# Experts of a routed MLP in steps of 256 tokens, layer 1 with the weights held still, instead of blocks of 128 tokens

## The chip, the cores and the metric

One core of one Trainium2 chip runs the whole program. The metric is the device time of one execution in microseconds (us); the time of a kernel is the median of several runs. Beside it one execution is profiled: its trace gives each instruction's engine, start and length. The engines are PE (TensorE; PEld is its loading of weights), DVE (VectorE), ACT (ScalarE), POOL (GpSimd) and SP, which only issues transfers.

## The reference

Three parts follow each other: attention, a plain MLP, and an MLP of eight experts, of which each token uses one. The change is in the last and at its seam to the second.

```python
def _moe_ref(x, w_in, w_out):                       # 2304 x 512, hidden 2048
    r = np.maximum(x @ w_in, 0.0)
    return (r * r) @ w_out

def _moe2_ref(x, expert_emb, tau, w1, w2):          # 8 experts, 512 -> 1024 -> 512
    xn, en = x / norm(x), expert_emb / norm(expert_emb)
    logits = xn @ en.T / tau
    expert_idx = np.argmax(logits, axis=1)
    gate_w = softmax(logits)[arange(N), expert_idx]
    for e in range(E):
        mask = expert_idx == e
        h = np.maximum(x[mask] @ w1[e], 0.0)
        out[mask] = gate_w[mask, None] * (h @ w2[e])
```

The inputs are drawn with a fixed seed. Worked out with the reference, the tokens per expert are 676 (expert 4), 436 (5), 449 (7), 466 (0), 171 (1) and 106 (2); experts 3 and 6 get none. The kernel visits them in that order.

## The kernel before

**Numbers.** Every float32 product is made of three single-pass products of rounded halves: a tensor is split into a high part (`hh`, `xTh`, `Wh`), a rounded copy made by ACT, and a low part (`hl`, `xTl`, `Wl`), the difference made by DVE. "hi times hi, hi times lo, lo times hi" is why matmuls come in threes.

**The plain MLP, second half of its hidden layer.** Chunks `cc` of 256 tokens; the last chunk comes first, then 0 to 7. `layer1` (L680) holds a 128x128 piece of the weights still and streams 256 tokens through it, 12 matmuls a step; `layer2` (L714 to L716) holds the hidden values and streams 512 columns of weights, 6 matmuls a step. Each finished chunk is routed while the next one is computed (`route`): DVE works out the expert of each token, its place among that expert's tokens (`lj`), and POOL makes a one-hot table `L` of the places (L860). After four routed chunks `first_block` picks the expert with the most tokens so far as the first one, loads its weights, and collects the first 128 of its tokens into `xg[0]` with an indirect transfer (L922). PE transposes them five steps later (L927).

**Tables.** After the last chunk `tables` turns counts and places into lists of token numbers: DVE builds `Bk` and `rg`, PE multiplies them with `L` (L1047), and `T.idxg` tells the indirect transfers which rows to collect. A later part (L1107 to L1123, run at `next(gates)`, then L1127 on PE) makes the gate weight of each token the same way.

**Experts.** A block (`body`) is 128 tokens of one expert. With `xT` (the transposed tokens) held still, layer 1 streams `w1` in 24 matmuls of 512 columns (L1240) into two banks; ACT takes the ReLU into `h` (L1259, L1265); PE transposes `h` in two lots of four (L1229); ACT and DVE split it; layer 2 holds the transposed `h` and streams `w2` in 24 matmuls of 512 columns (L1250 to L1252). In between, four transposes of the next block's tokens (L1183). Each of the 21 blocks is stored with a DVE multiply by the gate (L1307) and an indirect transfer to the output (L1308). When the expert changes, 16 half pieces of weights are split by ACT and DVE (`own`, `ahead`), under conditions that each engine evaluates for itself. Two copies of the body stand in the program, one for each of two weight slots; PE, ACT and DVE run in the order of the code.

**Order of blocks 0 to 2.** Block 0 stands before the tables in PE's order only in part: the last chunk's routing and the tables lie among its matmuls. `next(gates)` is called after block 1.

Of the kernel before, what the change touches and what calls it, by code (L numbers as in the profile page):

```python
# [9 lines left out]
F32 = DT.float32  # L10
F32R = DT.float32r
BF16 = DT.bfloat16
I32 = DT.int32
# [17 lines left out]
NBLK = 25  # L31
NSURE = 18
# [26 lines left out]
TURN0 = 5  # L59
# [554 lines left out]
class Mlp:  # L614
# [158 lines left out]
    def routing(self, c, late, emb, tau):  # L773
# [8 lines left out]
        self.sq = c.tile([128, DM], BF16, name="sq")  # L782
# [18 lines left out]
    def route(self, cc, x2):  # L801
# [51 lines left out]
        V.tensor_reduce(rk, t16, AX.X, ALU.add)  # L853
        ri = c.tile([128, 2, 2], I32, name="ri", tag="ri")
# [17 lines left out]
    def first_block(self):  # L872
# [36 lines left out]
        for sl in spans:  # L909
            V.scalar_tensor_tensor(b0[:, sl], R.lj[:, 1, sl], 0.0, R.O[:, sl, 0], ALU.is_equal, ALU.mult)  # L910
            V.tensor_scalar_mul(rhs[:, sl, 0], b0[:, sl], R.iotap)
            V.tensor_tensor(rhs[:, sl, 1], b0[:, sl], R.iotat[:, sl, 0], ALU.mult)
        tab = R.ps.tile([128, 512], F32, name="tab0", tag="r")
        tiles = [t for sl in spans for t in range(sl.start, sl.stop)]
        for t in tiles:
            nc.tensor.matmul(tab[:, :2], R.L[:, t], rhs[:, t], start=t == tiles[0], stop=t == tiles[-1])
        p1 = c.tile([128, 1], F32, name="p1")
        V.tensor_scalar(p1, tab[:, 0:1], -1.0, None, ALU.add)
        idx = c.tile([128, 1], I32, name="idx0")
        V.scalar_tensor_tensor(idx, tab[:, 1:2], 128.0, p1, ALU.mult, ALU.add)  # L920
        m = len(tiles) * 128
        nc.gpsimd.indirect_dma_start(sh.xg[0], None, sh.x2d[:m], IO(ap=idx, axis=0), bounds_check=m - 1, oob_is_err=False)  # L922
        for _ in range(TURN0):
            yield
        pt = self.psr.tile([128, 512], F32, name="xt", tag="xt", bufs=2)
        for kc in range(4):
            nc.tensor.transpose(pt[:, kc * 128:kc * 128 + 128], sh.xg[0][:, kc * 128:kc * 128 + 128], sh.ident)  # L927
        sh.xT0 = [c.tile([128, DM], F32R, name=n) for n in ("xT0h", "xT0l")]
        split(nc, pt, *sh.xT0, nc.scalar, nc.vector)
        yield  # L930

# [30 lines left out]
def routing_setup(tc, sh, c):  # L962
# [20 lines left out]
    R.iotat = c.tile([128, NTT, NBLK], BF16, name="iotat")  # L983
    for a, n, base in ((0, NTT - 2, 2), (NTT - 2, 2, 0)):
        nc.gpsimd.iota(R.iotat[:, a:a + n], [[1, n], [0, NBLK]], base=base, channel_multiplier=0,
                       allow_small_or_imprecise_dtypes=True)

    R.two = c.tile([128, NBLK], I32, name="two")
    nc.gpsimd.iota(R.two, [[1, NBLK]], base=126, channel_multiplier=0)
# [8 lines left out]
def tables(ctx, tc, sh):  # L998
# [5 lines left out]
    T.idxg = c.tile([128, NBLK], I32, name="idxg")  # L1004
    T.idxs = c.tile([128, NBLK], I32, name="idxs")
    T.gate = c.tile([128, NBLK], F32, name="gate")
    T.meta = c.tile([128, NBLK + 4], I32, name="meta")
# [7 lines left out]
    V.tensor_scalar(ci, cnt[:, :E], 127.0, None, ALU.add)  # L1015
    V.tensor_scalar(ci, ci, 7, None, ALU.arith_shift_right)
# [4 lines left out]
    for t in cum:  # L1021
# [15 lines left out]
    V.tensor_tensor(sb, sb, R.lj[:, 1], ALU.add)  # L1037
    Bk = st.tile([128, NTT, NBLK], BF16, name="Bk")
    V.tensor_tensor(Bk, R.iota128[:, :NBLK].unsqueeze(1).to_broadcast([128, NTT, NBLK]),
                    sb.unsqueeze(2).to_broadcast([128, NTT, NBLK]), ALU.is_equal)  # L1040
    rg = st.tile([128, NTT, 3, NBLK], BF16, name="rg")
    rhs = rg[:, :, :2]
    V.tensor_scalar_mul(rhs[:, :, 0], Bk, R.iotap)
    V.tensor_tensor(rhs[:, :, 1], Bk, R.iotat, ALU.mult)
    tab = pst.tile([128, 512], F32, name="tab", tag="r")
    for i in range(NTT):
        nc.tensor.matmul(tab[:, :2 * NBLK], R.L[:, i], rhs[:, i].rearrange("p a b -> p (a b)"),  # L1047
                         start=i == 0, stop=i == NTT - 1)
    P1 = st.tile([128, NBLK], F32, name="P1")
    V.tensor_copy(P1, tab[:, :NBLK])  # L1050
    idx = st.tile([128, NBLK], F32, name="idx")
    V.scalar_tensor_tensor(idx, tab[:, NBLK:2 * NBLK], 128.0, P1, ALU.mult, ALU.add)
    first = V.tensor_scalar(T.idxg, idx, -1.0, 0.0, ALU.add, ALU.max)
    for s in range(1, 2):
        nc.gpsimd.indirect_dma_start(sh.xg[s], None, sh.x2d, IO(ap=T.idxg[:, s:s + 1], axis=0),
                                     bounds_check=NT - 1, oob_is_err=False)
    with tc.issue_after(first.ins):
        ge = st.tile([128, NBLK, E], F32, name="ge")
        V.tensor_tensor(ge, R.iota128[:, :NBLK].unsqueeze(2).to_broadcast([128, NBLK, E]),
                        cend.unsqueeze(1).to_broadcast([128, NBLK, E]), ALU.is_ge)  # L1060
        ex = st.tile([128, NBLK], F32, name="ex")
# [5 lines left out]
        V.tensor_tensor(ge, ge, used.unsqueeze(1).to_broadcast([128, NBLK, E]), ALU.mult)  # L1067
        at = st.tile([128, NBLK], F32, name="at")
# [3 lines left out]
        V.tensor_tensor(ge, at.unsqueeze(2).to_broadcast([128, NBLK, E]), rank.unsqueeze(1).to_broadcast([128, NBLK, E]),  # L1072
                        ALU.is_equal)
        flags = st.tile([128, 3, NBLK], F32, name="flags")
        V.memset(flags[:, :, 0], 0.0)
        more = st.tile([128, NBLK], F32, name="more")
        V.tensor_reduce(more, ge, AX.X, ALU.add)
        V.tensor_tensor(ge, ge, R.iota128[:, :E].unsqueeze(1).to_broadcast([128, NBLK, E]), ALU.mult)
        nx = st.tile([128, NBLK], F32, name="nx")
        V.tensor_reduce(nx, ge, AX.X, ALU.add)  # L1080
        e8 = st.tile([128, NBLK], I32, name="e8")
        V.tensor_scalar(e8, nx, R.e0, None, ALU.add)
        V.tensor_scalar(T.meta[:, :NBLK], e8, E - 1, None, ALU.bitwise_and)
# [8 lines left out]
        V.tensor_tensor(flags, flags, R.two.bitcast(F32).unsqueeze(1).to_broadcast([128, 3, NBLK]), ALU.mult)  # L1092
# [11 lines left out]
    with tc.issue_after(last.ins):  # L1104
# [29 lines left out]
def experts(tc, sh, gates, w1, w2, out):
    nc = tc.nc
    T = sh.T
    with ExitStack() as ctx:
        st = ctx.enter_context(tc.tile_pool(name="est", bufs=1, reuse_waits="tile"))
        psh = [sh.psm.tile([128, 512], F32, name=f"psh{j}", tag="y", bufs=2) for j in range(2)]
        pst = [sh.psm.tile([128, 512], F32, name="pst0", tag="L1", bufs=1)]  # L1140
        pst += [sh.psr.tile([128, 512], F32, name=f"pst{j}", tag="xt", bufs=2) for j in range(1, 3)]
        psy = [sh.psr.tile([128, 512], F32, name=f"psy{j}", tag="y", bufs=2) for j in range(2)]
        ident = sh.ident
# [3 lines left out]
        def ring(n, name, shape, dtype, tiles=(), used=0):  # L1147
            tiles = [*tiles] + [st.tile(shape, dtype, name=f"{name}{j}") for j in range(len(tiles), n)]
            turns = [used]
            rings.append(turns)  # L1150

            def take():
                turns[0] += 1
                return tiles[(turns[0] - 1) % n]
            return take

        new_xh = ring(2, "xTh", [128, DM], F32R, sh.xT0[:1], 1)
        new_xl = ring(2, "xTl", [128, DM], F32R, sh.xT0[1:], 1)
        new_h = ring(1, "h", [128, F], F32)
        new_hh = ring(2, "hh", [128, 512], F32R)  # L1160
        new_hl = ring(2, "hl", [128, 512], F32R)
        spare = sh.x1[NCH - 1].rearrange("p a b -> p (a b)")
        new_psh = ring(2, "psh", None, None, psh)
        new_pst = ring(3, "pst", None, None, pst)
        new_psy = ring(2, "psy", None, None, psy)

        xg, xT, hb = {}, {}, {}

        def gather(s):
            if s >= NBLK:  # L1170
                return
            t = sh.xg[s % 2]
            nc.gpsimd.indirect_dma_start(t, None, sh.x2d, IO(ap=T.idxg[:, s:s + 1], axis=0),  # L1173
                                         bounds_check=NT - 1, oob_is_err=False)
            xg[s] = t

        def turn_x(s):
            if s >= NBLK:
                return
            t = xg.pop(s)  # L1180
            pt = new_pst()
            for kc in range(4):
                nc.tensor.transpose(pt[:, kc * 128:kc * 128 + 128], t[:, kc * 128:kc * 128 + 128], ident)  # L1183
            hi = new_xh()
            lo = new_xl()
            xT[s] = (hi, lo)
            return split(nc, pt, hi, lo, nc.scalar, nc.vector)
# [251 lines left out]
```

## Time and profile before

| | |
|---|---|
| median of 3 runs | 978.58 us (978.37 to 980.16) |
| profiled execution, its own time | 976.67 us |
| its span in the trace | 974.7 us |
| PE busy | 924.9 us, 95% of the span |
| DVE, ACT, POOL busy | 63%, 57%, 29% |
| expert part, from the first layer 1 matmul | 691.9 us to the end |
| indirect stores | 21 |

A matmul's bar in the trace is longer than the time it takes its place in the row: the next one starts before the bar has ended. The cost of a matmul is read from the distance of the starts. Times below are us from the start of the span.

### The profile page before, as it was taken

The page shows a single profiled execution, that of the slowest core. Times are in us where ns is not written, and L with a number is a line of the kernel's source. Part 1 is how long each engine was busy: PE and PEld are TensorE (multiplying, and loading weights), DVE is VectorE, ACT ScalarE, POOL GpSimd, SP SyncE. Part 2 cuts the span into 40 slices and gives each one's busy share as a digit, 9 for nine tenths or more (in the row PEclk, how much of TensorE's full clock was granted, in tenths as well). Part 3 has the DMA queues.
Part 4 walks back from the last instruction along what each step waited for, and adds up shares of the span by engine and source line. Part 5 has one row for each costly group of instructions (what it writes and reads, how often), then busy time and mean ns, then how long its engine had stood idle before and what let it go on. Part 6 is the DMA issues. An engine that isn't in the chain of part 4 may idle for free. (4 is left out here: it accounts for less than half of the span.)

```text
span 974.7 us, 19052 instructions
## 1 busy us (share of the span) xinstructions
PE 924.9 (95%) x5864; PEld 772.3 (79%) x5864; DVE 615.6 (63%) x1741; ACT 553.8 (57%) x1425; POOL 278.6 (29%) x346
## 2 busy tenths in 40 slices
PE   7887798899999999999999999999989999999996
PEld 6666675688888888898888988898777878887875
DVE  4797768656676765488517778888642444444364
ACT  4676767677676766576655555664422434444353
POOL 4364554533333443101111112441412111111121
PEclk8999989899999999999999999999999999999998
DMA  6676655454444430254311112421061342425160
GB/s 165 148 177 149 156 138 143 99 127 94 117 95 115 95 85 2 67 171 154 109 44 44 64 46 92 158 66 44 23 218 46 92 154 85 173 73 185 66 204 28
DMA packets 106779, 105.10 MB, mean 108 GB/s; under 512 B 65967, under 2 KB 76207, under 8 KB 106624
## 3 DMA queue, kind: packets, MB, share of 16 engines
q1 hardware_dynamic: 101200, 90.17, 33.2%
q0 software_dynamic: 4224, 12.89, 3.9%
q8 instruction: 58, 0.95, 0.4%
q14 instruction: 97, 0.79, 0.3%
q10 hardware_dynamic: 1200, 0.30, 0.1%
HBM read 70.01 MB, written 14.43 MB: 87 GB/s over the span
## 5 line engine op out<-in xcount | busy, mean ns | idle before, releaser
L680 PE MATMUL ps<-xh,Wh 128*128 128x256 f32 x416 | 119.7, 288 | 0.0
L392 POOL TENSOR_SCALAR A<-A,sm,g 128x512 f32<-128x512 f32 (+4 forms) x108 | 75.4, 706 | 153.3 <-DVE sm L455 60.9
L680 PE MATMUL ps<-xl,Wh 128*128 128x256 f32 x416 | 118.3, 284 | 0.9 <-DVE xl L654 0.9
L680 PE MATMUL ps<-xh,Wl 128*128 128x256 f32 x416 | 118.1, 284 | 0.0
L714 PE MATMUL y<-Wh,gh 128*128 128x512 f32 x288 | 115.3, 400 | 0.1
L716 PE MATMUL y<-Wh,gl 128*128 128x512 f32 x288 | 113.6, 394 | 0.0
L715 PE MATMUL y<-Wl,gh 128*128 128x512 f32 x288 | 113.4, 394 | 0.0
L446 ACT ACTIVATE A<-A,nm 128x256 f32<-128x256 f32 (+2 forms) x144 | 80.3, 558 | 37.8 <-DVE nm L438 36.8
L690 DVE TENSOR_TENSOR gl<-r,gh 128x256 fp32r<-128x256 f32 x144 | 69.5, 483 | 46.2 <-ACT gh L689 41.7
L684 ACT ACTIVATE r<-ps 128x256 f32<-128x256 f32 x144 | 54.8, 380 | 76.5 <-PE ps L680 73.1
L438 DVE CUSTOM_DVE_ANT_0 A<-ps,mask 64x256 f32<-64x256 f32 (+4 forms) x160 | 75.5, 473 | 33.7 <-PE ps L431 30.9
L109 DVE TENSOR_TENSOR hl<-pst,hh 128x512 fp32r<-128x512 f32 x42 | 29.0, 691 | 104.4 <-ACTq L1215 93.6
L680 PEld LDWEIGHTS ps<-xh,Wh 128*128 128x128 f32 x416 | 79.7, 192 | 4.9 <-issue 1.9
L680 PEld LDWEIGHTS ps<-xl,Wh 128*128 128x128 f32 x416 | 79.8, 192 | 3.8 <-DVE xl L654 1.1
L680 PEld LDWEIGHTS ps<-xh,Wl 128*128 128x128 f32 x416 | 79.9, 192 | 0.0
L689 ACT CAST gh<-r 128x256 fp32r<-128x256 f32 x144 | 58.4, 405 | 37.6 <-PE y L715 35.5
L1308 POOL DMA_INDIRECT out_dram<-x,idxs x21 | 21.2, 1011 | 197.1 <-DVE x L1307 149.4
L1250 PE MATMUL psy<-Wh,hh 128*128 128x512 f32 x168 | 70.2, 418 | 0.0
L1252 PE MATMUL psy<-Wh,hl 128*128 128x512 f32 x168 | 66.8, 398 | 0.4 <-DVEq L1215 0.4
L108 ACT CAST Wh<-x 128x512 fp32r<-128x512 f32 x96 | 55.0, 618 | 20.5 <-SPq L1297 7.9
L1251 PE MATMUL psy<-Wl,hh 128*128 128x512 f32 x168 | 66.4, 395 | 0.0
L716 PEld LDWEIGHTS y<-Wh,gl 128*128 128x128 f32 x288 | 54.1, 188 | 13.6 <-DVE gl L690 0.7
(333 smaller groups left out, 2426.6 us busy)
## 6 DMA issues: line engine op xcount, KB each, us to landing
x<-in_moe_w_dram SPq DMA_DIRECT2D x48, 512.0 KB, 3.8
raw<-in_moe_w_in_dram SPq DMA_DIRECT2D x16, 512.0 KB, 4.1
raw<-in_moe_w_out_dram SPq DMA_DIRECT2D x16, 512.0 KB, 4.0
ks<-hk SPq DMA_DIRECT2D x60, 128.0 KB, 2.4
x2d<-x SPq DMA_DIRECT2D x18, 256.0 KB, 2.0
kn<-in_k_dram SPq DMA_DIRECT2D x32, 128.0 KB, 2.8
vn<-in_v_dram SPq DMA_DIRECT2D x32, 128.0 KB, 2.7
x2p<-x SPq DMA_DIRECT2D x16, 256.0 KB, 2.4
```

Of the source, the lines that this page charges most:

```text
L392: nc.gpsimd.tensor_scalar(A, A, a, b, ALU.mult, ALU.mult)
L438: nc.vector.tensor_tensor_reduce(A[rows, a:n], tiles[j][rows, :w], mask[rows, end - w:end], -1.0, 3e38, ALU.add, ALU.min, nm[rows, j:j + 1])
L446: nc.scalar.activation(A[:, a:a + w], src, AF.Exp, bias=nm[:, 0:1], scale=sign, accum_out=sm[:, i:i + 1])
L680: nc.tensor.matmul(ps[:, :CH], a, b, start=n == 0, stop=n == len(ops) - 1)
L689: self.later(3, "act", lambda: nc.scalar.copy(gh, r))
L690: self.later(3, "dve", lambda: nc.vector.tensor_tensor(gl, r, gh.bitcast(F32), ALU.subtract))
L714: nc.tensor.matmul(y, gh[:, sl], wh, start=first, stop=False)
L715: nc.tensor.matmul(y, gh[:, sl], wl, start=False, stop=False)
L716: nc.tensor.matmul(y, gl[:, sl], wh, start=False, stop=last)
L1250: nc.tensor.matmul(y, hh[:, sl], a, start=n == 0 and kc == 0, stop=False)
L1251: nc.tensor.matmul(y, hh[:, sl], b, start=False, stop=False)
L1252: nc.tensor.matmul(y, hl[:, sl], a, start=False, stop=n == 1 and kc == 3)
```

## The change

A step is now 256 tokens of one expert, two halves of 128. In layer 1 the pieces of `w1` are held still and the 256 transposed tokens stream through, so that `h` arrives transposed; ACT takes the ReLU straight into the high part, DVE the low part straight from the bank, and the transposes of `h`, the tile `h` and the copies of its transposes are gone. Layer 2 is as before, for two halves, into two fixed banks `y[0]` and `y[1]`. There is one pair of `xT` tiles instead of two in turn. Tables have 34 columns (17 steps of two halves) instead of 25; with the token counts above there are 3 + 2 + 2 + 2 + 1 + 1 = 11 steps instead of 6 + 4 + 4 + 4 + 2 + 1 = 21 blocks. The first step has both halves: `first_block` collects 128 tokens after four routed chunks and 128 more after seven (`SEEN`), transposed three MLP steps later. If the first expert had under 256 tokens by then, `hole` moves its later tokens on; with the inputs above it has 486 and `hole` is 0. `next(gates)` is now called ahead of step 0, and the conditions' words are read at the end of step 0.

```diff
-NBLK = 25
-NSURE = 18
+NST = 17
+NHB = 2 * NST
+NSURE = 9
+SEEN = 7
...
+        def fetch(half):
...
+            for t in tiles:
+                nc.tensor.matmul(tab[:, :2], R.L[:, t], rhs[:, t], start=t == tiles[0], stop=t == tiles[-1])
+            p1 = c.tile([128, 1], F32, name=f"p1_{half}")
+            V.tensor_scalar(p1, tab[:, 0:1], -1.0, None, ALU.add)
...
+            nc.gpsimd.indirect_dma_start(sh.xg[half], None, sh.x2d[:m], IO(ap=idx, axis=0), bounds_check=m - 1,
+                                         oob_is_err=False)
...
+        fetch(0)
         for _ in range(TURN0):
             yield
...
+        turn(0)
+        while R.count < SEEN:
+            yield
+        cnt = R.ps.tile([128, 512], F32, name="cnt", tag="r")
+        nc.tensor.matmul(cnt[:, :E], R.ones, R.Osum[:, SEEN - 1], start=True, stop=True)
+        V.tensor_scalar(R.hole[:, 0:1], cnt[:, 0:1], -1.0, float(CH), ALU.mult, ALU.add)
+        V.tensor_scalar_max(R.hole[:, 0:1], R.hole[:, 0:1], 0.0)
+        fetch(1)
+        for _ in range(TURN1):
+            yield
+        turn(1)
         yield
+
+
+def turned(nc, sh, pt, half):
+
+    for kc in range(4):
+        nc.tensor.transpose(pt[:, kc * 128:kc * 128 + 128], sh.xg[half][:, kc * 128:kc * 128 + 128], sh.ident)
+    hi, lo = (t[:, :, half * 128:half * 128 + 128] for t in sh.xT)
+    split(nc, pt.rearrange("p (k t) -> p k t", k=4), hi, lo, nc.scalar, nc.vector)
...
+            def layer1(g):
+                ps = new_bank().rearrange("p (a b) -> p a b", a=2)
+                for a in range(2):
+                    sl = slice((2 * g + a) * 128, (2 * g + a) * 128 + 128)
+                    for kc in range(4):
+                        for j, (w, x) in enumerate(((Wh, hi), (Wh, lo), (Wl, hi))):
+                            nc.tensor.matmul(ps[:, a], w[kc][:, sl], x[:, kc], start=kc + j == 0, stop=kc + j == 5)
+                hh, hl = hT[g] = new_hh(), new_hl()
+                nc.scalar.activation(hh, ps, AF.Relu)
+                nc.vector.scalar_tensor_tensor(hl, ps, 0.0, hh.bitcast(F32), ALU.max, ALU.subtract)
+
+            def layer2(g):
+                hh, hl = hT[g]
+                for a in range(2):
+                    wh, wl = Wh[4 + g][:, a * 512:a * 512 + 512], Wl[4 + g][:, a * 512:a * 512 + 512]
+                    for h in range(2):
+                        xh, xl = hh[:, a, h * 128:h * 128 + 128], hl[:, a, h * 128:h * 128 + 128]
+                        nc.tensor.matmul(y[h], xh, wh, start=g + a == 0, stop=False)
+                        nc.tensor.matmul(y[h], xh, wl, start=False, stop=False)
+                        nc.tensor.matmul(y[h], xl, wh, start=False, stop=g + a == 4)
+
+            own(4)
+            layer1(0)
+            own(5)
+            layer1(1)
+            own(6)
+            layer2(0)
+            own(7)
+            layer2(1)
+            if s == 0:
+                words["once"] = nc.values_load(T.once[0:1], engines=[ENG.Activation, ENG.DVE], min_val=0, max_val=1)
+            ahead(0)
+            layer1(2)
+            ahead(1)
+            layer1(3)
+            ahead(2)
+            layer2(2)
+            if s + 1 < NST:
+                for h in range(2):
+                    turned(nc, sh, pst[h], h)
+            ahead(3)
+            layer2(3)
...
         load(range(8), 0)
...
+        next(gates)
+        block(0)
         with tc.manual_schedule(engines={ENG.PE, *IN_ORDER}):
...
+            for h in range(2):
+                nc.scalar.copy(room(0, h), y[h])
+            block(1)
             next(gates, None)
```

**Three places in the engines' orders.** PE in the second half of an ordinary block, before (`h` is the tile of ReLU values, `xg` the collected tokens of the next block, `hh` and `hl` the split parts):

```order
L1229 MATMUL pst_9288<-ident,h_9294 128x128 x4
L1250 MATMUL psy_9290<-Wh_5_76,hh_9295 128x512
L1251 MATMUL psy_9290<-Wl_5_84,hh_9295 128x512
L1252 MATMUL psy_9290<-Wh_5_76,hl_9297 128x512
L1250 MATMUL psy_9290<-Wh_5_76,hh_9295 128x512
L1215 UNCONDITIONAL_BRANCH
L1221 UNCONDITIONAL_BRANCH
L1251 MATMUL psy_9290<-Wl_5_84,hh_9295 128x512
L1252 MATMUL psy_9290<-Wh_5_76,hl_9297 128x512
L1183 MATMUL pst_9289<-ident,xg_6593 128x128 x4
L1250 MATMUL psy_9290<-Wh_6_77,hh_9296 128x512
L1251 MATMUL psy_9290<-Wl_6_85,hh_9296 128x512
```

PE at the same point of an ordinary step, now:

```order
L1255 MATMUL psy_9340<-Wh_6_77,hh_9342 128x512
L1256 MATMUL psy_9340<-Wl_6_85,hh_9342 128x512
L1257 MATMUL psy_9340<-Wh_6_77,hl_9344 128x512
L961 MATMUL pst_9337<-ident,xg_6592 128x128 x4
L961 MATMUL pst_9338<-ident,xg_6593 128x128 x4
L1255 MATMUL psy_9339<-Wh_7_78,hh_9343 128x512
L1256 MATMUL psy_9339<-Wl_7_86,hh_9343 128x512
L1257 MATMUL psy_9339<-Wh_7_78,hl_9345 128x512
L1255 MATMUL psy_9340<-Wh_7_78,hh_9343 128x512
```

The transposes of `h` are gone, and those of the next tokens have become two lots, one for each half.

DVE around the gate weights, before: the low part of the next block's tokens (`xT0l`), then the conditions of the weight pieces, then the gate arithmetic between blocks 1 and 2.

```order
L109 TENSOR_TENSOR xT0l<-pst_9289,xT0h 128x512
L1221 COMPARE_AND_BRANCH
L109 TENSOR_TENSOR Wl_3_82<-x_3_93,Wh_3_74 128x512
L1221 UNCONDITIONAL_BRANCH x2
L1283 UNCONDITIONAL_BRANCH
L936 TENSOR_SCALAR sq<-ss 128x18
L937 TENSOR_SCALAR sq<-sq 128x18
L939 RECIPROCAL sq<-sq 128x18
L940 SCALAR_TENSOR_TENSOR sq<-sq,ss 128x18
L941 SCALAR_TENSOR_TENSOR sq<-sq 128x18
```

DVE near the end of step 0, now: the arithmetic of the gates (`gr`, `gp`, `rg`) stands around the low parts of both halves of step 1's tokens (`xTl`).

```order
L1153 TENSOR_TENSOR gr<-gt,gp 128x18
L1158 TENSOR_TENSOR rg<-Bk,gp 128x18x34
L1154 CAST gp<-gr 128x18
L111 TENSOR_TENSOR xTl<-pst_9337,xTh 128x4x128
L1234 COMPARE_AND_BRANCH
L111 TENSOR_TENSOR Wl_3_5685<-x_3_93,Wh_3_5677 128x512 x2
L1234 UNCONDITIONAL_BRANCH x2
L1155 TENSOR_TENSOR gr<-gr,gp 128x18
L1158 TENSOR_TENSOR rg<-Bk,gp 128x18x34
L1156 CAST gp<-gr 128x18
L111 TENSOR_TENSOR xTl<-pst_9338,xTh 128x4x128
L1158 TENSOR_TENSOR rg<-Bk,gp 128x18x34
```

The gate arithmetic has moved from between blocks 1 and 2 to in among the two `xTl`, which step 1's first matmuls read.

PE in the plain MLP just after the seventh chunk is routed, before (`gh` and `gl` are hidden values of the plain MLP):

```order
L680 MATMUL ps<-xh_8736,Wl_0_5682 128x256
L714 MATMUL y<-Wh_7_5681,gh 128x512
L715 MATMUL y<-Wl_7_5689,gh 128x512
L716 MATMUL y<-Wh_7_5681,gl 128x512
L714 MATMUL y<-Wh_7_5681,gh 128x512
```

and now, with the first of 14 matmuls of the second `fetch`:

```order
L682 MATMUL ps<-xh_8739,Wl_0_5682 128x256
L716 MATMUL y<-Wh_7_5681,gh 128x512
L717 MATMUL y<-Wl_7_5689,gh 128x512
L926 LDWEIGHTS L
L926 MATMUL tab_8844<-rhs_8043,L 128x2
```

What moved in is the table of the second half: it reads `rhs` and `L`, which DVE and POOL make from the seventh chunk's places.

## Rows read from the trace of the kernel before

**Rows 1.** The page, costliest groups: line, engine, operation, count, busy, mean ns.

```profile
L680 PEld LDWEIGHTS ps<-xh,Wh 128*128 128x128 f32 x416 | 79.7, 192 | 4.9 <-issue 1.9
...
L1308 POOL DMA_INDIRECT out_dram<-x,idxs x21 | 21.2, 1011 | 197.1 <-DVE x L1307 149.4
```

**Rows 2.** Windows: stretch, length, busy and count by engine, PEclk, DMA.

```profile
790.00:890.00 100.00, 99.24 (x478) 80.62 (x477) 41.88 (x64) 41.06 (x72) 17.42 (x16) 1.00 0.36 122
```

**Rows 3.** Timeline of PE in block 4: start, length, instruction, idle before.

```profile
752.49 0.40 PE L1240 MATMUL psh<-Wh,xT0h 128*128 128x512 f32 x1
...
756.23 0.39 PE L1240 MATMUL psh<-Wl,xT0h 128*128 128x512 f32 x1
756.46 0.60 PE L1229 MATMUL pst<-ident,h 128*128 128x128 f32 x4
...
757.13 0.39 PE L1240 MATMUL psh<-Wh,xT0h 128*128 128x512 f32 x1
```

**Rows 4.** Timeline of PE: the first layer 1 matmul of blocks 7 and 14.

```profile
790.20 0.40 PE L1240 MATMUL psh<-Wh,xTh 128*128 128x512 f32 x1
...
877.48 0.39 PE L1240 MATMUL psh<-Wh,xT0h 128*128 128x512 f32 x1
```

**Rows 5.** Timeline of PE: the first and last of 12 matmuls in the plain MLP.

```profile
677.64 0.28 PE L680 MATMUL ps<-xh,Wh 128*128 128x256 f32 x1
...
678.95 0.28 PE L680 MATMUL ps<-xh,Wl 128*128 128x256 f32 x1
```

**Rows 6.** PE's waits from 692 to 967: total us, times, longest.

```profile
PE pst L1183 <- DMA xg<-x2d,idxg: 2.3, 1, 2.3
PE pst L1229 <- ACT h L1259: 2.1, 4, 0.8
PE psh L1240 <- DVE lj L858: 0.8, 1, 0.8
PE psy L1252 <- DVEq L1215: 0.4, 1, 0.4
```

**Rows 7.** Windows after the wait for the tokens of block 1.

```profile
710.20:713.60 3.40, 3.40 (x10) 2.62 (x9) 2.21 (x9) 0.43 (x1) 0.60 (x1) 0.50 0.42 106
713.60:720.00 6.40, 6.40 (x31) 5.28 (x31) 0.69 (x1) 1.90 (x4) 0.00 (x0) 1.00 0.94 337
```

**Rows 8.** Timeline of PE in the same stretch.

```profile
710.38 0.63 PE L1250 MATMUL psy<-Wh,hh 128*128 128x512 f32 x1
...
712.93 0.63 PE L1240 MATMUL psh<-Wh,xTh 128*128 128x512 f32 x1
```

**Rows 9.** Timeline when the seventh chunk is routed.

```profile
666.16 0.18 PE L845 MATMUL pr<-O,tri 128*128 128x16 bf16 x1 [1.19 <-DVE O L840]
...
667.98 0.17 DVE L858 CAST lj<-ri 128x4 f32<-128x4 int32 x1
...
668.25 1.18 POOL L860 TENSOR_SCALAR L<-iota,lj 128x128 bf16<-128x128 f32 x2 [2.26 <-DVE lj L858]
```

**Rows 10.** Timeline in block 0: the table's 18 matmuls.

```profile
703.80 0.61 PE L1047 MATMUL tab<-rg,L 128*128 128x50 bf16 x18
```

**Rows 11.** Timeline of DVE: the gate arithmetic, its first and last rows.

```profile
727.25 0.18 DVE L1107 TENSOR_SCALAR ss<-ss 128x18 f32<-128x18 f32 x1
...
730.25 1.70 DVE L1123 TENSOR_TENSOR rg<-Bk,gp 128x450 bf16<-128x450 bf16 x3
```

**Rows 12.** Waits from 730 to 975: DVE's sequencer at a condition.

```profile
DVE xTl L109 <- DVEq L1221: 0.8, 5, 0.2
```

**Rows 13.** Timeline in block 4: the next block's tokens.

```profile
761.73 0.60 PE L1183 MATMUL pst<-ident,xg 128*128 128x128 f32 x4
...
762.37 0.59 ACT L108 CAST xTh<-pst 128x512 fp32r<-128x512 f32 x1 [1.18 <-PE pst L1183]
...
762.99 0.69 DVE L109 TENSOR_TENSOR xTl<-pst,xTh 128x512 fp32r<-128x512 f32 x1 [1.07 <-ACTq L1221]
```

**Rows 14.** Timeline of the end.

```profile
966.39 0.39 PE L1252 MATMUL psy<-Wh,hl 128*128 128x512 f32 x1
...
966.82 0.75 DVE L1307 TENSOR_SCALAR x<-psy,gate 128x512 f32<-128x512 f32 x1 [1.23 <-PE psy L1252]
...
967.85 1.01 POOL L1308 DMA_INDIRECT out_dram<-x,idxs  x1 [10.16 <-DVE x L1307]
```

More of the change, by code (lines that the diff above doesn't have):

```diff
@@ L56 @@
 STRICT, BUSY = 9, {-5: 14, 0: 12, 2: 6}
-TURN0 = 5
+TURN0, TURN1 = 5, 3
 ONPE = (NCH - 2,)
@@ L923, in first_block, with turn @@
+        def turn(half):
+            pt = self.psr.tile([128, 512], F32, name="xt", tag="xt", bufs=2)
+            turned(nc, sh, pt, half)
+        fetch(0)
         for _ in range(TURN0):
             yield
[L925 to L928, printed above, removed]
@@ L1177, in turn_x @@
[L1177 to L1187, printed above, removed]
+            for n in range(2):
+                nc.gpsimd.indirect_dma_start(sh.xg[n], None, sh.x2d, IO(ap=T.idxg[:, 2 * s + n:2 * s + n + 1], axis=0),
+                                             bounds_check=NT - 1, oob_is_err=False)
@@ L1278, in block, with arms @@
+            ahead(3)
+            layer2(3)
+        def arms(s, flag, *does):
+            kept = [list(r) for r in rings]
+            with tc.If(bit(words[flag], s) < 1) as cmp, tc.manual_schedule(engines=IN_ORDER | {ENG.PE}):
+                does[0]()
+            for r, was in zip(rings, kept):
+                r[:] = was
+            with cmp.Else(), tc.manual_schedule(engines=IN_ORDER | {ENG.PE}):
+                does[1]()
         def block(s):
-            kept = [list(r) for r in rings], dict(xg), dict(xT)
@@ L1293, in block @@
-            if s + 1 < NBLK:
-                with tc.If(bit(more, s + 1) > 0):
+                body(0, 0)
+                words["odd"] = word(0, [ENG.PE, ENG.Activation, ENG.DVE])
+                words["change"] = word(1, [ENG.Activation, ENG.DVE])
+                words["more"] = word(2, [ENG.SP])
+            else:
+                arms(s, "odd", lambda: body(s, 0), lambda: body(s, 1))
+            if s + 1 < NST:
+                with tc.If(bit(words["more"], s + 1) > 0):
                     load(range(4), s + 1)
@@ L1296, in block @@
             if s:
-                with tc.If(bit(more, s) > 0):
+                with tc.If(bit(words["more"], s) > 0):
                     load(range(4, 8), s)
             gather(s + 2)
-            return y
-        def room(s):
-            return spare[:, s % 2 * DM:s % 2 * DM + DM]
-        def store(s, y):
-            ob = room(s)
-            nc.vector.tensor_scalar_mul(ob, y, T.gate[:, s:s + 1])
-            nc.gpsimd.indirect_dma_start(out, IO(ap=T.idxs[:, s:s + 1], axis=0), ob, None,
-                                         bounds_check=NT - 1, oob_is_err=False)
@@ L1311, in experts, with room, store @@
-        xT[0] = sh.xT0
-        xg[1] = sh.xg[1]
+        def room(s, h):
+            return rooms[s % 2][:, h * DM:h * DM + DM]
+        def store(s, src):
+            for h in range(2):
+                ob, c = room(s, h), 2 * s + h
+                nc.vector.tensor_scalar_mul(ob, src[h], T.gate[:, c:c + 1])
+                nc.gpsimd.indirect_dma_start(out, IO(ap=T.idxs[:, c:c + 1], axis=0), ob, None,
+                                             bounds_check=NT - 1, oob_is_err=False)
         load(range(8), 0)
-        once = nc.values_load(T.once[0:1], engines=[ENG.PE, ENG.Activation, ENG.DVE], min_val=0, max_val=1)
@@ L1315, in experts @@
-        change = word(1, [ENG.Activation, ENG.DVE])
-        more = word(2, [ENG.SP])
-        y = block(0)
+        next(gates)
+        block(0)
         with tc.manual_schedule(engines={ENG.PE, *IN_ORDER}):
-            nc.scalar.copy(room(0), y)
-            y = block(1)
-            nc.scalar.copy(room(1), y)
-            next(gates)
-            odd = word(0, [ENG.PE, ENG.Activation, ENG.DVE])
-            y = block(2)
-            next(gates, None)
-        store(0, room(0))
-        store(1, room(1))
@@ L1334, in experts @@
         with ExitStack() as ifs:
-            for s in range(NSURE, NBLK):
+            for s in range(NSURE, NST):
                 ifs.enter_context(tc.If(nbv > s))
-                store(s, block(s))
+                block(s)
+                store(s, y)
 @with_exitstack
@@ L1404, in tile_kernel @@
             pass
+        for _ in sh.R.first:
+            pass
     gates = tables(ctx, tc, sh)
```

258 lines of the change are left out of this document (96 added, 162 removed).

## The prediction

> **What bounds the kernel now.** I read the windows first. In a long stretch of blocks PE is busy 99 us of 100 at the full granted clock, the other engines less than half [rows 2]. So time there is what PE's own instructions need, plus the few waits, and the question is how many instructions of which kind a token costs. The timeline gives the price of each kind. Sixteen matmuls of 512 columns lie between 752.49 and 756.23, so one takes 0.234 us. From 756.23 to 757.13 there are two of them and four transposes; the four take 0.43 [rows 3]. A block is 48 matmuls and twelve transposes: 48 x 0.234 + 3 x 0.43 = 12.5. Seven blocks in a row took 87.28, 12.47 each [rows 4], so that sum is complete: branches between blocks cost PE nothing that can be seen.
>
> The list of PE's waits has what comes on top. In blocks 1 to 20 they are 2.1 us before the transposes of `h`, four times, and 0.4 once; in block 0 0.8 behind the last chunk's places and 2.3 behind the collected tokens of block 1 [rows 6]. A matmul's bar is 0.39 where its turn is 0.234, so each wait costs 0.16 more than is listed. After the 2.3 us the clock stood at half for one stretch [rows 7], where matmuls came 0.425 apart (six from 710.38 to 712.93, [rows 8]).
>
> **The change, part by part.**
>
> *Steps for blocks, -3.2.* Layer 1 of a step is 96 matmuls of 256 columns with weights still. The plain MLP has this form already: twelve of them lie 0.119 apart (1.31 over eleven, [rows 5]), the same 128x256 with a 128x128 load of the same type. So 96 x 0.119 = 11.43; layer 2 is 48 x 0.234 = 11.22; eight transposes 0.87: 23.52 a step. Eleven steps are 258.7; the 21 blocks of now, seen as 21 stores [rows 1], are 21 x 12.47 = 261.9. Taking out 16 of 24 transposes for 256 tokens is worth 1.7 a pair, but 0.2 goes to the narrower matmuls, and 22 halves are computed for 21 blocks, which takes back half a step.
>
> Narrow matmuls double the weight loads of layer 1. A load lasts 0.192 [rows 1], more than the 0.119 between matmuls, so it lies beside other matmuls and costs nothing. The Trainium skill says otherwise (TensorE: Matmul & The Clock Gate, Part 3, "The mechanism"): a load overlaps running matmuls only if it goes to other rows of the array, and here both use all 128. The trace does not agree: starts 0.119 apart with loads of 0.192 can't stand one behind the other. What it would cost if the rule held for the added loads is a rival below.
>
> *Waits in blocks 1 to 20, -3.3.* The 2.1 and 0.4, five times with 0.16 each. The longest ones come from ACT being late with the first ReLU, behind eight weight pieces at a change of expert. Now two pieces stand between ReLUs, and each ReLU (0.6) and low part (0.75, as the multiply in [rows 14]) has 24 matmuls, 2.86 us, to be done in. If that cover failed the 3.3 would come back. Bounds: 0 to 3.3.
>
> *Block 0's waits, -4.7.* 0.8 + 2.3 + 2 x 0.16 = 3.4, and seven matmuls at half clock, 7 x 0.19 = 1.3. They go because a full pair of tokens, 23.5 us of matmuls, now stands where 12.5 did: the table of step 1 and its two collections have ten more us. Bounds: 3.0 to 4.7.
>
> *Table of step 0, +0.6.* It lies in layer 2 of step 0 and needs three DVE operations that are now 34/25 as wide; three such took 1.70 [rows 11], so they grow by 0.6, and its 18 matmuls (0.61, [rows 10]) by at most 0.2. Part of it is covered. 0 to 1.2; I take the middle.
>
> *Start of step 1, +3.8.* This is a wait that the change makes. DVE's order puts the gate arithmetic ahead of and between the two `xTl`, where it stood behind them. From the last matmul of layer 1 in step 0: about 1.75 until the fourth `hl` is made (0.3, a ReLU 0.6, 0.75 and handovers). Then two small operations 0.42, the arithmetic from L1107 to the first `rg` 3.0 [rows 11], two `rg` of 0.57 x 34/25 = 0.77 each, three conditions of about 0.2 [rows 12], two `xTl` of 0.69 [rows 13]: 6.95, so 8.7 in all. PE has 24 matmuls of layer 2, eight transposes and one matmul of step 1 in that time, 5.62 + 0.87 + 0.12 = 6.6. It waits 2.1, and 2.5 if DVE comes half a us late from the table's arithmetic ahead of it, which I take. A wait of 2.3 was followed by half clock before, so 1.3 more. Bounds: 0 (other order of arrival, no slowdown) to 5.5 (DVE 1.5 later). The matmuls of step 1 are what stands behind it; reading the condition's word on PE falls into the same wait and is free there.
>
> *Second fetch in the plain MLP, +2.4.* After the seventh chunk's `pr` at 666.3 PE has twelve matmuls and two of layer 2 until the new table: 1.9, so it is there at 668.2. Its last one-hot `L` ends at 668.25 + 1.18 = 669.4 [rows 9], 669.7 with the two operations for `hole` ahead of `lj`. Wait 1.5. The 14 matmuls take 14/18 of 0.61, 0.5; four transposes 0.43. The other instructions queue on DVE (some ten of 0.2, one of 0.69) inside a chunk that had room. The transposes come some 6.5 us after the table (four large matmuls at 0.234 and two MLP steps of 12 x 0.119 + 6 x 0.234); until then three small operations on DVE, an issue of 1.01 on POOL [rows 14] and the landing must be done. No row prices that landing alone; I take it to fit, and the upper bound holds a miss of some 1.5. Bounds: 0.9 to 4 (the clock falls too).
>
> *End, +0.5.* The last step stores two halves: one more multiply of 0.75 and one more issue of 1.01 on POOL [rows 14], of which the first store's landing covers most, since expert 2 has 106 tokens and the second half is empty. 0 to 1.1.
>
> *At nothing.* One `xT` pair instead of two: layer 1 has read it long before it is rewritten. At a step's end the second half's cast ends 0.64 + 2 x 0.6 after the first transpose and its low part 0.75 later, 2.6, while PE has 0.87 + 2.81 + 0.12 = 3.8: 1.2 to spare; the rival below is about that. One pair of `y` banks: two multiplies of 0.75, needed 5.7 later. POOL issues the same number of halves and is busy 17 us of 100 [rows 2]. Weight transfers are as many as before and have twice the time per step.
>
> Sum: -3.2 - 3.3 - 4.7 + 0.6 + 3.8 + 2.4 + 0.5 = -3.9. The profiled execution spans 974.7 and took 976.67; it would span 970.8 and take 972.8. The median of the runs is 978.58, 1.9 above the profiled one; less 3.9 it is **974.7**.
>
> **Rivals.**
>
> *The gates don't hold step 1.* If DVE gets through faster than I add up, or the wait is short enough for the clock to stay, 3.8 goes: 970.9; with the MLP's wait gone too, 969.4. For it: the sum of small operations is long and each may overlap by 0.1. Against: two `rg` and both `xTl` alone are 2.9, in strict order. 17 in 100.
>
> *The step's seam waits (slower).* With one `xT` pair, the first matmuls of every step need both halves split. The chain has 1.2 to spare by rows of a contiguous 128x512 tile; it now writes 128x4x128 into half of a wider one, behind the weight pieces of `ahead(2)` at a change. From 1.6 of lateness on, ten seams eat the 3.9; at 2 they cost 8, 982.7. Against: 0.59 and 0.69 are per element, not per shape, and changes are five. 14 in 100.
>
> *A heavier start.* The clock falls after the MLP's wait as well (1.3), the table costs its upper bound (0.6), the gates hold step 1 a us longer: 977.6. 8 in 100.
>
> *Weight loads show.* By the rule named above, 48 added loads a step of 0.19 would be 9.1, some 100 in eleven steps: 1,075. The rows of the plain MLP speak against it as plainly as rows can. 2 in 100.
>
> *Not eleven steps.* One step more is 23.5: 998. It needs other counts than those of the inputs, and the 21 stores fit them. 3 in 100.
>
> **How the numbers follow.** My own sum has 56 in 100, with 972 to 977.5 for its bounds. The runs of this kernel differ by 0.2%, 2 us, so under 976.6 is faster and over 980.5 slower. Faster: 48 of the 56 and the 17 of the first rival, 0.65. Same: the other 8, the heavier start and 2 of the seam, 0.18. Slower: the rest, 0.17. The range 968.5 to 980.5 holds my case, the first rival, the heavier start and the mild end of the seam, some 83 in 100.
>
> **What will show it.** Right: 96 matmuls of layer 1 0.119 apart and steps of 23.5 from step 2 on; no wait before layer 2 at changes of expert; one wait of 2 to 3 at the start of step 1, ended by DVE's `xTl`, with half clock behind it; one of 1 to 2 at the second `fetch`, ended by POOL's `L`. Wrong: steps over 24.0 with waits for `xTl` at each start (the seam), starts over 0.13 apart in layer 1 (loads), 12 or more steps, or no wait at step 1.

## The result and the profile after

The changed kernel is slower by 1.3%: 992.14 us median (988.36 to 993.18, 4 runs) against 978.48 (978.17 to 980.16), a ratio of 1.0131 [1.0114, 1.0149]. Forecast were 974.7 and a range up to 980.5. The profiled execution spans 989.7 us, 15.0 more than that of before.

The kernel does what was meant to make it faster. Between waits a step takes 23.2 to 23.5 us (forecast 23.52), and in layer 1 a matmul follows the other after 0.11 to 0.12 (775.68, 775.79, 775.91 below), beside loads of 0.194 each (a row of the page of the profile):

```profile
L1244 PEld LDWEIGHTS psh<-xTh,Wh 128*128 128x128 f32 x352 | 68.3, 194 | 13.1 <-ACT Wh L110 7.3
```

The list of PE's waits from 640 us on (total, times, longest) shows what came instead:

```profile
PE psh L1244 <- ACT Wh L110: 6.4, 2, 3.4
PE psh L1244 <- issue: 4.6, 1, 4.6
PE pr L847 <- DVE O L842: 1.8, 2, 1.2
PE psh L1244 <- DVE xTl L111: 1.3, 1, 1.3
PE tab L926 <- POOL L L864: 0.3, 1, 0.3
```

Against [rows 6] the waits ahead of layer 2 are gone; three at the first matmul of a step (L1244) have come, 11.0 us in all, at steps 3, 7 and 10. In each a new expert starts. PE's timeline at the first of them (start, length, instruction, idle before; `psh` is a bank of layer 1, `psy` one of layer 2):

```profile
771.79 0.39 PE L1256 MATMUL psy<-Wl,hh 128*128 128x512 f32 x1
772.01 0.39 PE L1257 MATMUL psy<-Wh,hl 128*128 128x512 f32 x1
775.45 0.39 PE L1244 MATMUL psh<-xTh,Wh 128*128 128x256 f32 x1 [3.05 <-ACT Wh L110]
775.68 0.28 PE L1244 MATMUL psh<-xTl,Wh 128*128 128x256 f32 x1
775.79 0.28 PE L1244 MATMUL psh<-xTh,Wl 128*128 128x256 f32 x1
775.91 0.28 PE L1244 MATMUL psh<-xTh,Wh 128*128 128x256 f32 x1
```

The releaser in brackets is an inference of the profile, and a misleading one. The matmul reads piece 0 of the weights, which ACT had split by 757.3, 18 us earlier; the ACT instruction named is a piece of layer 2 (773.85 to 775.0), which only happened to end in the gap:

```profile
756.15 1.14 ACT L110 CAST Wh<-x 128x512 fp32r<-128x512 f32 x2 [0.57 <-ACTq L1229]
...
773.85 1.14 ACT L110 CAST Wh<-x 128x512 fp32r<-128x512 f32 x2 [2.49 <-SPq L1303]
```

The third wait says "issue": no releaser at all. Behind two of the waits PE's clock falls; windows of steps 7 and 10, with the granted share of 2.4 GHz (PEclk) as the third number from the right:

```profile
872.60:876.10 3.50, 3.50 (x19) 3.50 (x18) 0.00 (x0) 0.00 (x0) 0.25 (x1) 0.51 0.16 60
947.70:954.60 6.90, 5.89 (x27) 5.89 (x28) 0.00 (x0) 0.32 (x1) 0.99 (x1) 0.51 0.05 16
```

The other loss is at the end. PE's last matmul and POOL's last stores, where before had one store 1.07 behind PE [rows 14] and 7.9 us from PE's end to the end:

```profile
974.62 0.40 PE L1257 MATMUL psy<-Wh,hl 128*128 128x512 f32 x1
...
975.39 1.03 POOL L1314 DMA_INDIRECT out_dram<-x,idxs  x1 [0.97 <-DVE x L1313]
980.52 0.99 POOL L1314 DMA_INDIRECT out_dram<-x,idxs  x1 [4.10 <-DVEq L1331]
```

The second half's sums are multiplied by the gate by 975.8, but its store is issued at 980.5. From PE's end at 975.0 the program takes 14.7 us.

### The profile page after: what moved, and what is told of

It is laid out like the page before. It is cut to its first block, busy times and chain, and to the rows that moved or that the text cites. A ratio compares the mean times of both kernels' runs of the same rounds, so it can differ in the third digit from the quotient of the medians.

```text
span 989.7 us, 19061 instructions
## 1 busy us (share of the span) xinstructions
PE 924.9 (93%) x6295; PEld 797.6 (81%) x6295; DVE 617.9 (62%) x1760; ACT 529.2 (53%) x1387; POOL 281.0 (28%) x351
## 3 DMA queue, kind: packets, MB, share of 16 engines
q8 instruction: 64, 1.05, 0.5%
## 5 line engine op out<-in xcount | busy, mean ns | idle before, releaser
L718 PE MATMUL y<-Wh,gl 128*128 128x512 f32 x288 | 113.7, 395 | 0.0
L1244 PE MATMUL psh<-xTh,Wh 128*128 128x256 f32 x352 | 101.3, 288 | 11.0 <-ACT Wh L110 6.4
L1246 ACT ACTIVATE hh<-psh 128x512 fp32r<-128x512 f32 x44 | 26.3, 598 | 152.8 <-PE psh L1244 118.1
L1247 DVE SCALAR_TENSOR_TENSOR hl<-psh,hh 128x512 fp32r<-128x512 f32 x44 | 30.4, 690 | 115.9 <-ACT hh L1246 54.0
L1244 PE MATMUL psh<-xTl,Wh 128*128 128x256 f32 x352 | 100.7, 286 | 1.3 <-DVE xTl L111 1.3
L1244 PE MATMUL psh<-xTh,Wl 128*128 128x256 f32 x352 | 100.6, 286 | 0.0
L1244 PEld LDWEIGHTS psh<-xTh,Wh 128*128 128x128 f32 x352 | 68.3, 194 | 13.1 <-ACT Wh L110 7.3
L1244 PEld LDWEIGHTS psh<-xTl,Wh 128*128 128x128 f32 x352 | 68.2, 194 | 2.3 <-DVE xTl L111 1.6
```

The lines of the kernel that those rows point to most:

```text
L718: nc.tensor.matmul(y, gl[:, sl], wh, start=False, stop=last)
L1244: nc.tensor.matmul(ps[:, a], w[kc][:, sl], x[:, kc], start=kc + j == 0, stop=kc + j == 5)
L1247: nc.vector.scalar_tensor_tensor(hl, ps, 0.0, hh.bitcast(F32), ALU.max, ALU.subtract)
```

## The experiments

**Whose waits are those at steps 3, 7 and 10?** A seam is the change from one step to the next, an arm one side of a step's condition. One thing tells these seams from the others: they go from slot 0 to slot 1. In PE's program each step is two arms, slot 0 first, 152 matmuls (96 + 48 + 8) each with its load. A seam that stays in its slot branches over one arm. One from slot 1 to slot 0 falls straight on (steps 5 and 9, also changes of expert, no wait). One from slot 0 to slot 1 passes the rest of its own step and the first arm of the next: two arms, 304 matmuls, in two branches. Theory J: PE must then fetch instructions that it has not read ahead. Theory W takes the profile at its word: the new weights are late. First, the arms of step 2 alone change places (`swap2`):

```diff
 def arms(s, flag, *does):
+    swap = s in (2,)
+    does = does[::-1] if swap else does
...
-    with tc.If(bit(words[flag], s) < 1) as cmp, ...
+    w = bit(words[flag], s)
+    with tc.If(w > 0 if swap else w < 1) as cmp, ...
```

> The two arms of step 2 change places in the program (slot 1 first); nothing else. Theory J (a branch over two arms makes PE fetch its instructions anew): the step 1 to 2 seam now jumps over two arms and the step 2 to 3 seam over one, so a PE wait of 3 to 4 us appears at the first matmul of step 2 (about 749 us), where no expert changes, and the wait of 3.2 at the start of step 3 goes; the waits of 3.5 and 4.8 at steps 7 and 10 stay, the total stays within 2 us of 992. Theory W (the new expert's weight pieces come late, as the profile's list of waits says): no wait at step 2, and 3.2 stays at step 3.

Measured 989.7 (985.9 to 993.5, 2 runs). The wait moved, to a step in which no expert changes; step 3 starts at once (777.42 to 777.65):

```profile
749.03 0.72 PE L1162 MATMUL tg<-rg,L 128*128 128x102 bf16 x12
752.84 0.39 PE L1244 MATMUL psh<-xTh,Wh 128*128 128x256 f32 x1 [3.08 <-issue]
...
777.42 0.39 PE L1257 MATMUL psy<-Wh,hl 128*128 128x512 f32 x1
777.65 0.28 PE L1244 MATMUL psh<-xTh,Wh 128*128 128x256 f32 x1
```

W is refuted: it has no wait where no expert changes, and it keeps the one at step 3. Then the same swap for all steps that run slot 1, `s in (3, 4, 7, 8, 10)`, so that no seam passes two arms:

> The arms change places in steps 3, 4, 7, 8 and 10, those that these inputs run in slot 1, so that no seam jumps over two arms. Theory J: the three waits (3.2 + 3.5 + 4.8 = 11.5 us) and the stretches at half clock behind two of them (some 3 us) go: 976 to 980. Theory W: the weight pieces come as late as before, the waits stay, 990 to 993.

Measured 979.75 (976.5 to 984.5, 10 runs), ratio 1.001 [0.999, 1.003]. The three waits go, as J says, but seams over one arm now wait at steps 3, 5 and 10 in the profiled run, 0.4 to 1.7 each, and the ten runs scatter over 8 us:

```profile
PE psh L1244 <- issue: 2.2, 2, 1.7
...
PE psh L1244 <- ACT Wh L110: 0.4, 1, 0.4
```

One arm is near the edge. A version that doesn't lean on these token counts cuts the arms instead (`half_arms`): two conditions a step, each over 72 or 80 matmuls.

```diff
-arms(s, "odd", lambda: body(s, 0), lambda: body(s, 1))
+for p in range(2):    # own(4) .. layer2(1), then ahead(0) .. layer2(3)
+    arms(s, "odd", lambda: body(s, 0, (p,)), lambda: body(s, 1, (p,)))
```

> Each step's arms are cut in two after the second part of layer 2: two conditions a step, each over an arm of half the length. Theory J: a change into slot 1 now jumps over two half arms, the length that the other seams jump over without a wait, so the three waits and the half clock go as with the arms swapped: 976 to 980. Theory W: waits stay, 990 to 994, a little more for ten more conditions on three engines.

Measured **974.91** (974.4 to 975.3, 4 runs), ratio 0.9951 [0.9935, 0.9968]: 17 us under the kernel after and 0.5% under before. No matmul or instruction of the arithmetic is different; the listed waits that are left:

```profile
PE pr L847 <- DVE O L842: 1.8, 2, 1.2
PE psh L1245 <- DVE xTl L111: 1.3, 1, 1.3
PE tab L926 <- POOL L L864: 0.3, 1, 0.3
```

Steps 2 to 9, seam after seam, are one block of busy PE in its windows:

```profile
748.12:771.37 23.25, 23.25 (x156) 21.23 (x154) 11.61 (x21) 7.70 (x14) 8.85 (x8) 1.00 0.45 141
771.37:794.80 23.43, 23.43 (x153) 21.19 (x152) 10.88 (x18) 7.71 (x14) 4.41 (x4) 1.00 0.48 159
794.80:934.60 139.80, 139.80 (x914) 127.05 (x912) 66.22 (x104) 51.26 (x94) 24.54 (x24) 1.00 0.41 135
```

Cutting also adds conditions, so length itself was turned up again: whole arms in steps 3 and 7 alone (`joined`). Their seams branch over half an arm of 80 and a whole one.

```diff
+for p in ([(0, 1)] if s in (3, 7) else [(0,), (1,)]):
```

> Half arms, but with the whole arms of the kernel after in steps 3 and 7 alone. The seams 2 to 3 and 6 to 7 then branch over half an arm and a whole one, 1.5 arms (1 with half arms, no wait; 2 in the kernel after, waits of 3.2 and 3.5). If the length decides, waits come back at steps 3 and 7, of up to 3.5 us, and none at step 10: 975 to 983. If it takes two whole arms, no wait: 974.9.

Measured 979.64 (977.2 to 983.0, 8 runs). The waits are back at those two seams and no other, at half the size:

```profile
770.75 0.39 PE L1258 MATMUL psy<-Wh,hl 128*128 128x512 f32 x1
772.65 0.38 PE L1245 MATMUL psh<-xTh,Wh 128*128 128x256 f32 x1 [1.51 <-issue]
...
865.75 0.39 PE L1258 MATMUL psy<-Wh,hl 128*128 128x512 f32 x1
867.67 0.39 PE L1245 MATMUL psh<-xTh,Wh 128*128 128x256 f32 x1 [1.54 <-issue]
```

| matmuls that the longest kind of seam passes over | extra time at it, us |
|---|---|
| 120 (before, blocks 13 to 14, inside the stretch of [rows 4]) | none |
| 152 (after, seams that stay in a slot) | none |
| 152 (half arms) | none |
| 152 (arms swapped) | 0.5 to 1.9 at three seams, else none |
| 232 (joined) | 1.7, 1.7 |
| 304 (after) | 3.2, 3.5, 4.8 |
| 304 (swap2) | 3.2, 3.4, 4.9 |
| 304 (one_store, below) | 6.3, 3.3, 4.8 |

That it is a fetch, the transfers show. The view of DMA queues, cut to 773.00 to 774.10 inside the first wait of the kernel after, has one packet of 16 KB (the page of the profile: 64 packets, 1.05 MB) on an instruction queue; from 772.05 to 773.00 and from 774.10 to 775.45 that queue has none:

```profile
q8 instruction: 1, 0.02, 5.6%
```

In all eleven such waits of the kernels after, swap2, joined and one_store PE starts 1.4 to 1.9 us after such a packet has landed. Whose queue it is, counting tells. In the plain MLP, where PE has no branch in the trace, the ten stretches between two of its landings (484 to 680 us) hold 238 to 272 of PE's matmuls and loads, 254 on average, and 8 to 76 of DVE's operations. Two of the ten as windows (counts of PE, PEld and DVE in brackets; both ends cut through instructions):

```profile
522.12:541.85 19.73, 19.73 (x129) 17.63 (x128) 13.72 (x46) 10.91 (x29) 4.03 (x6) 1.00 0.16 54
600.79:620.43 19.64, 19.64 (x135) 17.61 (x134) 17.73 (x76) 10.71 (x29) 3.12 (x4) 1.00 0.66 229
```

So the queue brings PE's program, and a whole arm (152 matmuls and their loads) is 1.2 packets of it, half an arm 0.6.

The branches themselves stand in the records of PE's sequencer, and they show what the table's first column leaves out: no branch passes over 304 matmuls, two of 152 follow each other. Ahead of step 3 the kernel after has them at 768.85 (over the second arm of step 2) and 772.07 (over the first arm of step 3), each with a packet behind it (landed at 770.46 and 774.03). The sequencer is ahead of the engine: PE still works for 3.4 us after the first branch of a seam (4.2 at step 2 of swap2, with a table's matmuls there). A wait is what the seam takes beyond that: 6.6 to 9.7 us from the first branch to the next matmul with two whole arms, 5.1 in `joined`, 3.9 to 5.3 at the three seams of `swap_all`. So one branch over a whole arm can stop the sequencer as well (744.77 to 748.38 ahead of step 2 in the kernel after), while PE works on. Why others over one arm pass in 0.5 us (842.19 to 842.73) was not tested.

The Trainium skill has the rule (Runtime: NRT & Kernel Launch, "Instruction fetch mechanics"): an engine reads its instructions ahead in sequence, and a taken branch to a place outside that window forces a transfer before it can go on. These runs agree, with 3.2 to 6.3 us of waiting at the seams of 304 matmuls.

**The end.** In these inputs the last half (expert 2, second 128 tokens) is empty; `one_store` is the kernel after without that store:

```diff
-for h in range(2):
+for h in range(1 if s == 10 else 2):
```

> The last step (expert 2, 106 tokens) stores only its first half; the second half is empty in these inputs. If the second indirect store waits for the first to land, the tail behind PE's last matmul shrinks from 14.7 to 8.5 to 9.5 us and the time by 5 to 6 to some 986.5. If the end is a fixed cost of closing the program, or the first landing alone ends it, the time stays at 991 to 993.

Measured 990.74 (987.8 to 992.2), ratio 1.0104 [1.0082, 1.0126]; its runs and those of the kernel after overlap, and the waits above differ from one execution to the next (3.2 at step 3 there, 6.3 here). Its trace is clear: PE ends at 978.0, the program at 989.8, a tail of 11.8 instead of 14.7. So the second store costs 2.9, half of the expected 5 to 6. The other 3.9 over before's 7.9 remain, with one store as before, issued 0.4 behind PE:

```profile
978.36 1.02 POOL L1314 DMA_INDIRECT out_dram<-x,idxs  x1 [0.96 <-DVE x L1313]
```

In the records of POOL's sequencer, the closing of the program begins 0.2 after the issue of the last store in before (967.85, 968.05), and 4.5 after it here (978.36, 982.87), behind waits for transfers: the landing of the last store came 3.5 behind the start of the closing in before (971.52) and comes ahead of it here (982.67). Which of the twice as many stores and collections makes it wait was not tested. On the kernel with half arms, the same was tried in a form that holds for any inputs, the second half's store from step 9 on under a condition that the half has a token (`skip_empty`: a word loaded by POOL, and an `If` around the store):

> On the kernel with half arms: from step 9 on the second half's store is issued under a condition that the half has a token; in these inputs the last one is skipped. If the second store costs the end 2.9 us as in one_store: 972.0. If the condition's word and branches cost as much as the store (a load of 0.3 and the bookkeeping of the skipped store): 974 to 975.5.

Measured 974.86 (970.4 to 976.7, 7 runs), ratio 0.9952 [0.9933, 0.9971]. The tail is 12.2 instead of 14.5, but the median is that of half_arms, as was expected if the condition costs what it saves. The profiled execution, the slowest of the seven, reached the expert part 2.8 us later than that of half_arms and lost 1.5 in step 0 to half clock; whether the others did is not known, so what the condition is worth in time stays open. Doing the first half's six last matmuls ahead of the second's (`tail_order`: in the last `layer2`, `h` outside and `a` inside):

> On the kernel with half arms: the last six-and-six matmuls of layer 2 run half by half, so that the first half's sums are done six matmuls (1.4 us) earlier. Theory S (the end is a chain: multiply, store, its landing, second store, closing): the chain starts 1.4 earlier and the tail behind PE's last matmul goes from 14.5 to 13.1: 973.5. Theory F (the end hangs on the second half's sums or on closing alone): 974.9.

Measured 975.23 (973.7 to 978.5), tail 14.7. The first half's sums were three matmuls ahead already, so at most 0.7 was to be had, not the 1.4 expected; the first store came 0.4 earlier against PE's end, since `xTl` of the next step held DVE, and its landing took 0.7 longer. No gain; theory S is not refuted, its lever is too short.

**The start of step 1.** `gates_mid`, on half arms: `next(gates)` moves from ahead of `block(0)` to between the two halves of step 1.

> On the kernel with half arms (974.9): the gate arithmetic stands between the two halves of step 1 instead of ahead of step 0's end. Theory G (the gate arithmetic ahead of and between the two xTl holds step 1): PE's wait of 1.3 us for xTl at the start of step 1 goes and none comes at step 2: some 973.4. Theory X (the collected tokens or their high part are late there anyway): the wait stays, 974.9.

Measured 973.93 (972.3 to 975.3), ratio 0.9944 [0.9925, 0.9963]. The wait for `xTl` is gone and none has come: step 1 takes 24.0 instead of 25.6. In the profiled run step 0 fell to half clock for 3.4 us and gave 1.5 back, and the runs overlap with those of half_arms. The wait's cause (theory G) is shown; its worth in time is not, here or below: `best1`, which has this and the next change, lies 0.3 under `fetch_late` alone.

**The second fetch.** `fetch_late`, on half arms: one more `yield` ahead of it.

> On the kernel with half arms: the second fetch stands one step of the plain MLP (2.8 us) later. If the waits of 0.26 and 0.33 there are for the seventh chunk's places and its last one-hot, they go: 974.3. If the collected tokens are then late for their transposes (three steps later), a wait of up to 2 us comes there: 975 to 977.

Measured 973.74 (973.2 to 975.4), ratio 0.9948 [0.9932, 0.9965]. Both waits are gone and no other has come; from the seventh chunk's `pr` to step 0 it is 26.8 instead of 27.6.

**Together.** `best1` is half arms, `gates_mid` and `fetch_late`; `best2` has `skip_empty` as well.

> Half arms, the gate arithmetic between the halves of step 1, and the second fetch one step later, together. If the three are independent: 974.9 less 1.5 (wait for xTl) less 0.6 to 0.9 (waits at the second fetch), 972.5. If the start of the expert part falls to half clock in some executions as in gates_mid (1.5 us longer there), 973 to 974.

> As best1, and the second half's store from step 9 on under a condition. The tail was 12.2 instead of 14.5 us in skip_empty: 970.2 if that holds; 972 to 973.5 if the condition's bookkeeping costs elsewhere what it saves.

Measured 973.42 (971.0 to 974.1), ratio 0.9938 [0.9925, 0.9951], and **971.17** (969.2 to 975.1), ratio 0.9921 [0.9902, 0.9940]. The tails are 14.9 and 11.9, so the skipped store takes 3.0 off in these two traces; the runs overlap. All that PE waits for in `best2` from 640 us on is `O`, DVE's one-hot table of the tokens' experts, of two chunks. The 1.2 stood in before as well [rows 9], the 0.6 did not:

```profile
PE pr L847 <- DVE O L842: 1.8, 2, 1.2
```

Step starts in the traces (first matmul of layer 1 to that of the next step), us:

| step | 0 | 1 | 2 | 3 | 4 | 5 | 6 | 7 | 8 | 9 |
|---|---|---|---|---|---|---|---|---|---|---|
| after | 27.8 | 25.6 | 26.5 | 23.5 | 23.4 | 23.2 | 26.7 | 25.1 | 23.4 | 28.0 |
| swap2 | 27.8 | 28.8 | 24.8 | 23.4 | 23.4 | 23.2 | 26.5 | 26.3 | 23.4 | 28.1 |
| joined | 27.8 | 25.6 | 24.9 | 23.6 | 23.4 | 23.2 | 24.9 | 23.5 | 23.4 | 23.2 |
| half_arms | 27.8 | 25.6 | 23.3 | 23.4 | 23.4 | 23.2 | 23.2 | 23.4 | 23.4 | 23.2 |
| best1 | 27.8 | 24.0 | 23.3 | 23.4 | 23.4 | 23.2 | 23.2 | 23.4 | 23.4 | 23.2 |

## Why the prediction was wrong

**The step that failed** is in its first part: "Seven blocks in a row took 87.28, 12.47 each, so that sum is complete: branches between blocks cost PE nothing that can be seen." True for arms of 60 matmuls; it was carried over to arms of 152 without asking what a branch passes over, and the branches entered the sum at nothing. No rival covered it: the seam rival was about data (`xT`). It cost 11.5 us of gaps and, by the lengths of steps 7 and 10 against half_arms (25.1 to 23.4; 26.3 to 23.6 up to PE's end), 4.3 of half clock.

Term by term, the change in the span, profiled after against profiled before:

| term | forecast | measured |
|---|---|---|
| steps for blocks (23.31 a step in half_arms, not 23.52) | -3.2 | -5.1 over steps 2 to 10 |
| waits in blocks 1 to 20 | -3.3 | -3.3, none is left |
| block 0, its table, second fetch: from `pr` to step 1 | 56.1 in all | 55.4 in all |
| start of step 1 | +3.8 | +1.5 |
| branches over two arms, half clock behind them | 0 | +11.5, +4.3 |
| end | +0.5 | +6.8 |
| ahead of the changed part (`pr` at 668.06, not 666.16) | 0 | +1.9 |

The 56.1 is the 59.4 of before (666.16 to 725.56) less two blocks, plus a step of 23.31, with -4.7, +0.6 and +2.4 of the forecast. The differences from the forecast add up to 19.1; the span was 18.9 over the 970.8 that was forecast. The last row is not shown to be an effect of the change: 1.8 of it stands already at the first matmul of the plain MLP (113.7 against 111.9), and the variants, which have the same program there, reach that matmul at 111.9 to 115.2 and `pr` at 666.8 to 670.0.

- *Steps, waits at changes of expert, weight loads:* right. The rival that weight loads show fell, with starts of 0.11 to 0.12 apart.
- *Block 0's waits:* nearly right. The 0.8 behind the last chunk's places and the 2.3 behind the collected tokens went; a new one of 0.6 came at the last chunk's `pr` (701.25).
- *Second fetch:* right in kind, too long. The wait for `L` is 0.3 and one of 0.26 ahead of `cnt` (668.87) was not foreseen; a wait of 1.5 had been forecast. No half clock followed.
- *Start of step 1:* right in mechanism, shown by `gates_mid`; the wait is 1.3 in the list, 1.5 in turn, not 2.5, and the 1.3 for the clock did not come. The rival "the gates don't hold step 1" was the half-way case.
- *End:* the term was mis-sized by 6.3, and its reason was upside down. The first store's landing doesn't cover the second store, the second waits for it, 4.3 between 975.39 and 979.7, and without the second the tail is 2.9 shorter (one_store). For the other 3.9, a closing that now comes behind the last landing, the sum had no term.
- *Seam with one `xT` pair:* did not happen; half_arms shows no wait for `xTl` at any seam but step 1's.

That half_arms lands on the forecast 974.7 is partly chance: it has the end's +6.3, which the shorter steps and the smaller waits pay for in part.

## What to carry to other kernels

Where code stands in conditional arms, price an edit that lengthens them by what the taken branches pass over, in the worst case (two in a row, from the end of one first arm to the second arm of the next) and against the work that the engine still has when its sequencer meets the first, not by what branches cost at the old length; cutting each arm in two took back 17 us here at no visible cost. When a wait's named releaser worked on something that the waiting instruction doesn't read, or the row says "issue", look at the instruction queues before believing it, and move the code, not the data, to test it. A store that was alone at the end of a program is not free to become two: here both went to one tensor, and the second was issued only after the first had landed.

## What the runs showed of the hardware

Where two branches of PE, each over 152 matmuls and their loads, followed each other, PE stopped for 3.2 to 4.9 us (once 6.3); over 80 and then 152 for 1.7; over 152 once mostly not at all (0.5 to 1.9 at three seams of `swap_all`), and at no seam in the seven traces with half arms. PE's sequencer met the first branch 3.4 us before PE's work ran out, and PE went on 1.4 to 1.9 us after a 16 KB instruction packet had landed; such a packet lasts PE some 254 matmuls and loads. The length of the stop varies with the execution (3.2 and 6.3 at the same seam of the kernel after and one_store). The runs of kernels with such stops spread over 4 to 8 us, but so do some without (half_arms 0.8 over four runs, `tail_order` 4.7 over ten, `skip_empty` 6.3 over seven), so the spread is not shown to come from them. Behind seven of the nine gaps of 3.2 to 6.3 us PE's clock was then granted at half (1.2 GHz) for 3.4 or 6.8 us; behind two of them (3.2 in the kernel after, 3.3 in one_store) it stayed at 2.4 GHz, and so it did behind all of 1.5 to 1.7.
